# Block stack of sliding-window attention and a gated MLP: the opening loads, statistics and first tiles rearranged

## The chip, the cores and the metric

The kernel runs on one core of a Trainium2 chip. The metric is the device time of one execution in microseconds; lower is better. A core has five engines that are used here: TensorE (PE in the profile; its weight loads are the row PEld), VectorE (DVE), ScalarE (ACT), GpSimd (POOL) and SyncE (SP), which issues most of the transfers. Each engine works through its own list of instructions in order and waits on semaphores for the others.

## The reference

One layer norm feeds two branches, and their results meet at the end. S is 2048, D is 576, F is 4608, there are 32 heads of 18, and a query sees the last 256 keys.

```python
xn = _layernorm(x, axis=-1)            # eps = 1e-5, no scale or offset
s = _A_ref(xn, A_wqkv, A_wo)           # causal attention in a window of 256, 32 heads
g = _silu(_B_ref(xn, B_w_gate, B_w_up, B_w_down))
return x + s * g
...
# in _B_ref
g = jnp.einsum("bsd,df->bsf", x, w_gate)
u = jnp.einsum("bsd,df->bsf", x, w_up)
h = _sigmoid(g) * u
return jnp.einsum("bsf,fd->bsd", h, w_down)
```

## The kernel before

*Tiling.* The 2048 rows are four chunks of 512, each four blocks of 128 rows. D is split into a remainder of 64 and four pieces of 128. Every product runs as a pair of matmuls, one on rows 0 to 63 and one on rows 64 to 127 of the array (`pair`, line 123; `turn`, line 131). The gate and up projections of an F tile (128 columns of 4608, 36 tiles) are two operations: `f10` with the four large pieces and half the rows, `f11` with the other half and the remainder, which completes both sums.

*A planner sets the order.* The program first builds a graph of operations (`build_graph`, line 365). `schedule` (line 1125) then walks through time with an estimate for each operation, for the landing of each transfer and for the hand-over between engines, and picks for each engine the operation that can start soonest, a priority counting 10 ns a step (`PRIO_NS`). The list that results is what each engine runs; semaphores alone decide when. So a changed estimate changes the order of instructions, also far from the place where it is used. Attention (scores, exp, the product with V), the projections and the gate/up and down matmuls of several chunks are interleaved on TensorE in this way.

*The opening of chunk 0.* SP issues the four x blocks (`load_x`, line 418), then the gate and up weights of the first two F tiles (`wgs`, 256 columns each) and their remainders of 64 rows (`wgr`, 512 columns, for four tiles), then further weights. For each block the layer norm (`build_ln`, line 525) takes two half-row statistics on DVE (lines 541 and 543), aggregates them (545), adds eps (547), takes the power -0.5 on POOL (549), normalises on DVE (557), and copies 64 columns a second time (561), since the remainder is held twice. Ten small transposes on TensorE (`tr`, line 613) bring the block into PSUM, and one copy (590) into `xnT`. Block 2 has its statistics on ACT and POOL instead (`act_stats`, lines 600 to 604): a sum, a mean on POOL, a Square with that mean as bias, and again POOL. The PSUM copies of blocks 0, 1 and 2 are on ACT, that of block 3 on DVE (`XE_ENG`).

*Warm-up and early tiles.* TensorE runs 43 pairs of matmuls on zeros before the first transposes and ten more behind them (`warm`, line 490). The first two F tiles are early ones (`NEARLY`): each is computed in four slices of 128 columns of xnT, as the blocks come in; the first half of a third tile is held ready in a further PSUM unit (`ahead`, line 995).

*Runs.* The product with V (`f_pv`, line 804) runs for four groups of heads at a time as one unbroken run of 128 (chunk 0) or 192 small matmuls (the other chunks, line 817), eight runs in all. `fits` (line 1113) tells the planner where such a run may stand: it counts TensorE's instructions in blocks of 256 (`FETCH`), and asks that the time since the edge of the block before is at least `FETCH_NS`.

*Names.* `dma:x{i}` is the load of x block i, `dma:w:{c}:{wg}` that of a gate or up weight pair in chunk c, `dma:wgr` that of a remainder, `ln:*` the layer norm, `xe:{i}` the copy of block i from PSUM to `xnT`, `th` and `hm` the tanh and the product behind gate and up.

## Time and profile before

| what | value |
|---|---|
| median of the runs | 557.37 us (three: 557.37, 556.61, 557.46) |
| the profiled execution | 556.48 us; span from its first to its last instruction 555.2 us |
| granted TensorE clock in that execution | 1.00 |
| DMA | 75.87 MB, of which the queue of SP 68.71 MB |
| instructions fetched by the queue named instruction | 66 packets of 1.08 MB together (q8) |

The span is cut by the profile into forty slices for its busy digits. TensorE's are 8 in the first and the last slice and 9 in all others. In the first four slices the transfers run at 230 to 263 GB/s. Matmul rows overlap one another, because a matmul starts before the one ahead of it has left the array, so the distance from start to start tells more than the duration of a row. In a row of the timeline the first number is the start in us from the span's start, the second the duration, and what stands in brackets is the idle time of the engine before it and what ended that.

### The profile page before, as it was taken

How to read it: one execution, taken by the hardware profiler on the slowest of the kernel's cores; microseconds unless marked ns; L12 is line 12 of the kernel's file. 1: busy time of each engine (PE TensorE's matmuls, PEld its weight loads, DVE VectorE, ACT ScalarE, POOL GpSimd, SP SyncE). 2: the span in 40 equal slices, each digit the busy share in tenths (PEclk: the TensorE clock that was granted, in tenths of full speed). 3: DMA queues.
4: the chain of work that ended last, by engine and by line, in shares of the span. 5: the costliest groups of instructions: out<-in, count | busy, mean ns of one | idle time of the engine just before them, and what ended most of it. 6: DMA issues, size and time to landing. Idle time of an engine off the chain costs nothing.

```text
span 555.2 us, 19412 instructions
## 1 busy us (share of the span) xinstructions
PE 549.9 (99%) x8342; PEld 341.2 (61%) x8342; DVE 325.1 (59%) x782; ACT 271.7 (49%) x379; POOL 208.8 (38%) x360
## 2 busy tenths in 40 slices
PE   8999999999999999999999999999999999999998
PEld 7454455777555655577855565447877655445887
DVE  5467677745966545746565557664455657653511
ACT  4246554432566543645265563764165555765021
POOL 5634353826271230554452322745063332700300
DMA  8899999542256664462126653663013464540001
GB/s 230 234 263 239 248 241 257 150 91 59 72 164 182 198 167 132 129 161 53 32 65 193 201 162 101 185 179 87 9 34 103 119 204 138 153 134 2 20 28 46
DMA packets 141213, 75.87 MB, mean 137 GB/s; under 512 B 43676, under 2 KB 139260, under 8 KB 141128
## 3 DMA queue, kind: packets, MB, share of 16 engines
q1 hardware_dynamic: 133704, 68.71, 47.3%
q0 software_dynamic: 7424, 5.92, 4.0%
q8 instruction: 66, 1.08, 0.8%
q14 instruction: 19, 0.16, 0.1%
HBM read 63.18 MB, written 2.36 MB: 118 GB/s over the span
## 4 chain that ended last, share of the span: by engine, by line
PE 98%; DMA 1%; SPq 0%; issue 0%; DVE 0%; ACT 0%
PE ps L127 95%; PE ps L817 3%; DMA wgs<-in_B_w_up_dram 1%; SPq L290 0%; ACT thf L1087 0%; PE ps L613 0%; DVE thf L1089 0%; DVE xf L1092 0%
## 5 line engine op out<-in xcount | busy, mean ns | idle before, releaser
L127 PE MATMUL ps<-xnT,wgs 64*128 64x512 bf16 (+1 forms) x2400 | 284.0, 368 | 0.6 <-DMA wgs<-in_B_w_up_dram 0.5
L767 ACT ACTIVATE expr<-ps 128x1024 bf16<-128x1024 f32 (+4 forms) x160 | 155.0, 968 | 81.0 <-PE ps L127 80.5
L127 PEld LDWEIGHTS ps<-xnT,wgs 64*128 64x128 bf16 x2400 | 114.7, 94 | 108.6 <-issue 1.1
L127 PE MATMUL ps<-wd_sb,hT 64*128 64x288 bf16 (+2 forms) x2448 | 152.7, 276 | 0.0
L290 POOL DMA_DIRECT2D qk<-qd x160 | 82.9, 524 | 161.7 <-PE ps L127 152.9
L977 DVE SCALAR_TENSOR_TENSOR hT<-tring,ps 128x512 bf16<-128x512 bf16 x144 | 98.6, 685 | 74.2 <-ACT tring L974 72.6
L974 ACT ACTIVATE tring<-ps 128x512 bf16<-128x512 f32 x144 | 86.2, 598 | 113.9 <-PE ps L127 112.3
L127 PEld LDWEIGHTS ps<-wd_sb,hT 64*128 64x128 bf16 x2448 | 113.0, 94 | 29.4
L780 DVE TENSOR_TENSOR expr<-expr,mask 128x128 bf16<-128x128 bf16 (+2 forms) x240 | 65.2, 299 | 62.0 <-ACT expr L767 59.4
L290 POOL DMA_DIRECT2D oT<-o2T x72 | 36.8, 520 | 115.3 <-DVE ot L848 52.4
L731 POOL TENSOR_SCALAR kx<-kprev,small 128x256 bf16<-128x256 bf16 x64 | 60.1, 949 | 6.0 <-PE ps L127 5.1
L127 PE MATMUL ps<-qk,kx 64*128 64x320 bf16 (+1 forms) x704 | 59.2, 254 | 0.0
L127 PE MATMUL ps<-xnT,wgr 64*128 64x512 bf16 (+1 forms) x300 | 56.0, 367 | 0.0
L127 PEld LDWEIGHTS ps<-qk,kx 64*128 64x128 bf16 x704 | 31.9, 94 | 26.6
L127 PE MATMUL ps<-xnT,wqg 64*128 64x512 bf16 (+1 forms) x320 | 37.7, 355 | 0.0
L652 DVE CAST qd<-ps 128x1024 bf16<-128x1024 f32 (+1 forms) x20 | 22.3, 1115 | 11.1 <-PE ps L127 11.1
L845 DVE STREAM_TRANSPOSE ot<-ps 128x512 f32<-128x512 f32 x32 | 20.3, 687 | 13.9 <-PE ps L817 13.8
L127 PEld LDWEIGHTS ps<-xnT,wgr 64*128 64x128 bf16 x300 | 15.0, 94 | 16.4
L731 DVE TENSOR_SCALAR kx<-qk,small 128x512 bf16<-128x512 bf16 x64 | 21.9, 370 | 5.4 <-PE ps L127 4.9
L853 DVE STREAM_TRANSPOSE o2T<-o 128x512 bf16<-128x512 bf16 x32 | 22.6, 706 | 3.0 <-DMA oT<-o2T 2.5
L127 PEld LDWEIGHTS ps<-xnT,wqg 64*128 64x128 bf16 x320 | 15.0, 94 | 11.5 <-issue 0.4
L1080 ACT ACTIVATE thf<-ps 128x576 bf16<-128x576 f32 x12 | 7.8, 650 | 27.4 <-PE ps L127 27.4
(68 smaller groups left out, 289.3 us busy)
## 6 DMA issues: line engine op xcount, KB each, us to landing
wgs<-in_B_w_gate_dram SPq DMA_DIRECT2D x72, 256.0 KB, 3.5
wgs<-in_B_w_up_dram SPq DMA_DIRECT2D x72, 256.0 KB, 4.0
wd_sb<-in_B_w_down_dram SPq DMA_DIRECT2D x9, 576.0 KB, 6.7
wqg<-in_A_wqkv_dram SPq DMA_DIRECT2D x32, 128.0 KB, 3.8
qk<-qd POOLq DMA_DIRECT2D x100, 36.0 KB, 2.7
wgr<-in_B_w_gate_dram SPq DMA_DIRECT2D x36, 64.0 KB, 3.1
wgr<-in_B_w_up_dram SPq DMA_DIRECT2D x36, 64.0 KB, 2.9
wvo<-in_A_wqkv_dram SPq DMA_DIRECT2D x4, 576.0 KB, 4.2
```

The lines of the kernel that those rows point to most:

```text
L127: res = eng.matmul(outs[i], lhs(ROWS[t], i), rhs(ROWS[t], i), start=start, stop=stop, tile_position=(64 * t, 0))
L290: o = self.op(eng, DMA_ISSUE_NS[eng], lambda e: e.dma_start(dst, src), name, deps, prio, nbytes=nbytes)
L652: return eng.tensor_copy(dst, self.both(h, n))
L731: return e.tensor_scalar(self.kx[:, sx, pos:pos + n_ // SW, t, :], src.rearrange("p (s k) -> p s k", k=SW), self.half[:, t:t + 1], None, A ...
L767: return eng.activation(self.expr[:, se, :, lo * SW:NT], self.both(h, NT)[:, :, lo * SW:NT], ACTF.Exp, scale=SM_SCALE)
L780: return eng.tensor_tensor(e_, e_, m_, ALU.mult)
L817: res = eng.matmul(outs[i][p0:p0 + VH, cols], self.v_aug[ROWS[i], o:o + VH], self.expr[ROWS[i], se, t, cols], start=m == 0, stop=m == len( ...
L845: return e.transpose(self.ot1[:, p1, :], self.halves(hp, NT, un)[i])
L853: t2 = op("DVE", dve_ns(NT), lambda e, p2=p2, p3=p3: e.transpose(self.o2T[:, p3, :], self.o2[:, p2, :]), f"ot2:{c}:{pr}:{i}", deps=[on, d3 ...
L974: th = op("ACT", act_ns(NT), lambda e: e.activation(self.tring[:, st, :], bank(h, 0), ACTF.Tanh, scale=0.5), f"th:{c}:{ft}", deps=[pg, dt_ ...
L977: mu = op("DVE", dve_ns(NT), lambda e: e.scalar_tensor_tensor(self.hT[:, ft, :], self.tring[:, st, :], 1.0, bank(h, 1), ALU.add, ALU.mult) ...
L1080: th = op("ACT", act_ns(w), lambda e: e.activation(v2(t), y2(), ACTF.Tanh, scale=0.25), f"fth:{nm}", deps=[f2, dt_], prio=0)
```

## The change

- x block 0 is loaded in two transfers of 288 columns; blocks 1 and 2 follow; block 3 is issued behind the first gate and up weights and the first half of their remainder. That remainder is loaded in two halves of 256 columns.
- In chunk 0 (blocks 0, 1 and 3) eps is no longer added on DVE to the variance. GpSimd adds 576 eps to an entry of the first half's statistics before the aggregation, while DVE takes the second half.
- Block 2's statistics on ACT: the sum is taken with sign -1, and the Square uses it as its bias with scale 576, so that it needs nothing from POOL.
- The PSUM copy of block 0 moves from ACT to DVE.
- 41 warm-up pairs in place of 43, and none behind the first transposes.
- Three early F tiles in place of two; the third in slices of 384 and 128 columns. The held first half is that of the fourth tile, in a PSUM unit of its own (`pool_a`, unit 0).
- The planner: landing times of the opening's transfers come from a running count of bytes; some hand-over times, gaps between scores (`SPACE_NS`) and fill times differ; `fits` counts the time of a run from when the instructions before it could be taken up, with other bounds for three phases (`FETCH_NS`, `RUN_NEED`). So instructions change places in the whole program; TensorE has 24 warm-up matmuls fewer and 18 more for the slices of the third tile.

The core of the diff:

```diff
@@ -43,8 +43,12 @@
 FETCH = 256
 FETCH_AT = 193
 FETCH_AHEAD = 64
-FETCH_NS = (6200.0, 4350.0)
+FETCH_LEAD = 16
+QUEUED = 48
+FETCH_NS = (7800.0, 5700.0, 4250.0)
+RUN_NEED = (1.0, 1.0, 1.15, 1.0, 1.15, 1.0, 1.15, 1.0)
 RUN_NS = 6.3
+RELAX_NS = 100e3
 STEP_NS = (54.0, 30.6)
...
@@ -66,18 +70,24 @@
 NTH = 4
 NTAIL = 80
 LAST_STORES = 3
-LN_PRIO = (0, 0, 0, 16)
-X_PRIO = (0, 0, 0, 0)
-REM_PRIO = 0.6
+LN_PRIO = (10,0,10,60)
+X_PRIO = (0,.1,.2,.3,1.5)
+REM_PRIO = 0.3
+REM1_PRIO = 1.5
+LATE_PRIO = 1.9
+SPLIT = False
 STATS_ACT = (2,)
-APPLY_ACT = ()
 DUP_ACT = ()
-XE_ENG = ("ACT", "ACT", "ACT", "DVE")
-NWARM = (43, 10)
-NEARLY = 2
-FIRST_SLACK_NS = (-800.0, -1500.0)
+XE_ENG = ('DVE','ACT','ACT','DVE')
+NWARM = ((41,1),)
+HOLD = False
+NEARLY = 3
+OPEN_NS = 2000.0
+OPEN_BYTES_PER_NS = 270.0
+X_LAT_NS = (400.0, 400.0, 600.0, 700.0, 800.0)
+W_LAT_NS = (700.0, 800.0)
 BUSY_SLACK_NS = 1500.0
-PARTS = (((0, 1), (1, 2), (2, 3), (3, 4)),) * NEARLY
+PARTS = (((0, 1), (1, 2), (2, 3), (3, 4)),) * 2 + (((0, 3), (3, 4)),)
 NQK = 5
 
 DMA_ISSUE_NS = {"SP": 640.0, "POOL": 520.0, "ACT": 650.0}
...
@@ -88,10 +98,11 @@
 TURN_WAIT_NS = 235.0
 PE_OUT_NS = 210.0
 PE_IN_NS = 60.0
-POOL_IN_NS = 140.0
+POOL_IN_NS = 100.0
 DMA_PE_NS = 690.0
-FILL_NS = 100.0
-SPACE_NS = (1700, 1800, 1700, 1700)
+OPEN_PE_NS = 150.0
+FILL_NS = 80.0
+SPACE_NS = (1700, 2100, 1700, 2000)
 DMA_BYTES_PER_NS = 280.0
...
@@ -417,10 +430,13 @@
 
     def load_x(self, c, i=0):
         if c == 0:
-            for i in range(BPC):
-                self.x_dma[i] = (self.dma(self.x0[:, i, :], self.x[i * P:(i + 1) * P, :], P * D * 2, f"dma:x{i}", ("x0", i), prio=X_PRIO[i]),
-                                 self.x0[:, i, :])
-                self.x_dma[i][0].slack = -220.0
+            for n in range(BPC + 1):
+                i = max(n - 1, 0)
+                cs = slice(0, D) if n > 1 else slice(n * D // 2, (n + 1) * D // 2)
+                o = self.dma(self.x0[:, i, cs], self.x[i * P:(i + 1) * P, cs], P * (cs.stop - cs.start) * 2, f"dma:x{i}:{n}",
+                             ("x0", n), prio=X_PRIO[n])
+                o.lat = X_LAT_NS[n]
+                self.x_dma.setdefault(i, ([], self.x0[:, i, :]))[0].append(o)
             return
...
@@ -461,7 +477,9 @@
                          deps=[z], prio=0)
         self.warm_h = self.pool_f.hold()
         self.warm_src = zero
-        self.warm(NWARM[0], z, None, 107)
+        self.warm_last = None
+        for n, wide in NWARM:
+            self.warm(n, wide, z, self.warm_last, 100)
 
...
@@ -538,16 +556,17 @@
                 mean, rs = self.act_stats(x_in, o_x, pr)
                 ag = None
             else:
-                b1 = op("DVE", 390, lambda e, ss=ss, x_in=x_in: e.bn_stats(self.bnst[:, ss, 0, :], x_in[:, 0:288]),
-                        f"ln:bn1:{st}", deps=[o_x, ds], prio=pr)
-                b2 = op("DVE", 390, lambda e, ss=ss, x_in=x_in: e.bn_stats(self.bnst[:, ss, 1, :], x_in[:, 288:576]),
-                        f"ln:bn2:{st}", deps=[o_x, ds], prio=pr)
-                ag = op("DVE", 200, lambda e, ss=ss: e.bn_aggr(self.mv[:, ss, :], self.bnst[:, ss, :, :]),
-                        f"ln:ag:{st}", deps=[b1, b2], prio=pr)
-                ve = op("DVE", 140, lambda e, ss=ss: e.tensor_scalar(self.veps[:, ss, :], self.mv[:, ss, 1:2], EPS, None,
-                                                                    ALU.add), f"ln:ve:{st}", deps=[ag], prio=pr)
-                rs = op("POOL", 560, lambda e, ss=ss: e.tensor_tensor(self.rstd[:, ss, :], self.veps[:, ss, :],
-                                                                      self.neghalf[:, :], ALU.pow),
+                bs = self.bnst[:, ss, :, :]
+                b1, b2 = (op("DVE", 440, lambda e, bs=bs, x_in=x_in, n=n: e.bn_stats(bs[:, n, :], x_in[:, n * D // 2:(n + 1) * D // 2]),
+                             f"ln:bn{n}:{st}", deps=[o_x[min(n, len(o_x) - 1)], ds], prio=pr) for n in range(2))
+                var = self.mv[:, ss, 1:2]
+                if c == 0:
+                    b1 = op("POOL", 230, lambda e, bs=bs: e.tensor_scalar(bs[:, 0, 2:3], bs[:, 0, 2:3], EPS * D, None, ALU.add), f"ln:ep:{st}",
+                            deps=[b1], prio=pr)
+                ag = ve = op("DVE", 210, lambda e, ss=ss, bs=bs: e.bn_aggr(self.mv[:, ss, :], bs), f"ln:ag:{st}", deps=[b1, b2], prio=pr)
+                if c:
+                    ve = op("DVE", 140, lambda e, var=var: e.tensor_scalar(var, var, EPS, None, ALU.add), f"ln:ve:{st}", deps=[ag], prio=pr)
...
@@ -582,8 +595,6 @@
                 return self.transposes(eng, h, lambda r, o: self.xnr[r, sn, o:o + P])
             tr = op("PE", KB * 29.5, f_tr, f"tr:{st}", deps=[ap, dup, self.op_ident, war], prio=0, acq=h, ni=20)
             self.r_xn.release(sn, tr)
-            if i == 0:
-                self.warm(NWARM[1], None, tr, 80)
 
...
@@ -597,11 +608,11 @@
         op = self.op
         junk = self.tring[:, :, :].rearrange("p t n -> p (t n)")[:, 0:D]
         sx, nm, sq, ve = (self.act_st[:, k:k + 1] for k in range(4))
-        a1 = op("ACT", act_ns(D) + 150, lambda e: e.activation(junk, x_in, ACTF.Identity, accum_out=sx), "ln:as", deps=[o_x, self.op_tab], prio=pr)
-        m = op("POOL", 150, lambda e: e.tensor_scalar(nm, sx, -1.0 / D, None, ALU.mult), "ln:am", deps=[a1], prio=pr)
-        a2 = op("ACT", act_ns(D) + 150, lambda e: e.activation(junk, x_in, ACTF.Square, bias=nm, accum_out=sq), "ln:aq", deps=[m], prio=pr)
-        v = op("POOL", 150, lambda e: e.tensor_scalar(ve, sq, 1.0 / D, EPS, ALU.mult, ALU.add), "ln:av", deps=[a2], prio=pr)
-        rs = op("POOL", 560, lambda e: e.tensor_tensor(self.arstd[:, :], ve, self.neghalf[:, :], ALU.pow), "ln:ar", deps=[v, self.op_negh], prio=pr)
+        a1 = op("ACT", act_ns(D) + 190, lambda e: e.activation(junk, x_in, ACTF.Identity, scale=-1.0, accum_out=sx), "ln:as", deps=[o_x, self.op_tab], prio=pr)
+        a2 = op("ACT", act_ns(D) + 290, lambda e: e.activation(junk, x_in, ACTF.Square, bias=sx, scale=float(D), accum_out=sq), "ln:aq", deps=[a1], prio=pr)
+        m = op("POOL", 230, lambda e: e.tensor_scalar(nm, sx, 1.0 / D, None, ALU.mult), "ln:am", deps=[a1], prio=pr)
+        v = op("POOL", 290, lambda e: e.tensor_scalar(ve, sq, 1.0 / D ** 3, EPS, ALU.mult, ALU.add), "ln:av", deps=[a2], prio=pr)
+        rs = op("POOL", 560, lambda e: e.tensor_tensor(self.arstd[:, :], ve, self.neghalf[:, :], ALU.pow), "ln:ar", deps=[v, m, self.op_negh], prio=pr)
         return nm, rs
...
+            by = [[self.load_nat(self.wgs[:, sw, :, i, a:b], w[:, fc][:, a:b], f"dma:w:{c}:{wg}:{a}", ("w", sw, i, a), pr + later, [dw, self.op_xnT[0][0] if HOLD and c == 0 and wg == 1 else None])
+                   for i, w in enumerate((self.wg, self.wu))] for a, b, later in cuts]
+            ds = [d for g in by for d in g]
             if wg % 2 == 0:
                 f8 = slice(wg * WG * P, (wg + 2) * WG * P)
                 sr, dr = self.r_wr.produce()
                 rslots[wg // 2] = sr
-                self.op_wgr[wg] = self.load_rem(self.wgr[:, sr, :], (self.wg[:, f8], self.wu[:, f8]), f"dma:wgr:{c}:{wg}",
-                                                ("wgr", sr), pr + (REM_PRIO if c == 0 and wg == 0 else -0.5), [dr])
-            rem = self.op_wgr[wg - wg % 2]
+                first = c == 0 and wg == 0
+                self.op_wgr[wg], self.op_wgr[wg + 1] = [
+                    self.load_rem(self.wgr[:, sr, a * P:b * P], [w[:, f8][:, a * P:b * P] for w in (self.wg, self.wu)], f"dma:wgr:{c}:{wg}:{a}",
+                                  ("wgr", sr, a), pr + late, [dr])
+                    for a, b, late in (((0, WG, REM_PRIO), (WG, 2 * WG, REM1_PRIO)) if first else ((0, 2 * WG, -0.5),))] * (1 if first else 2)
+            rem = self.op_wgr[wg]
...
@@ -992,7 +1009,7 @@
                 for part in range(len(PARTS[ft])):
                     lo = gate_up(ft, h, 0, None if part else h, part, [u])
                     if ft == early - 1 and part == len(PARTS[ft]) - 1:
-                        ahead = self.pool_f.hold()
+                        ahead = (self.pool_a if NEARLY > 2 else self.pool_f).hold()
...
@@ -1110,14 +1127,25 @@
             waits[key] = max(waits.get(key, -1), d.idx)
         return {key: v for key, v in waits.items() if known.get(key, -1) < v}
 
-    def fits(self, at, n, st, places, ffn):
+    def fits(self, at, o, st, places, now, rate, waited):
+        n = o.run
+        need = RUN_NEED[sum(int(v) << 1 - j for j, v in enumerate(o.name.split(":")[1:3]))]
         def when(p):
             if p < at:
-                return next(t0 + (p - a0) * w for a0, t0, w in reversed(places) if a0 <= p)
-            return st + TURN_NS + min(p - at, n) * RUN_NS + max(p - at - n, 0) * STEP_NS[ffn]
+                return next((t0 + (p - a0) * w, kind) for a0, t0, w, kind, held in reversed(places) if a0 <= p)
+            return st + TURN_NS + min(p - at, n) * RUN_NS + max(p - at - n, 0) * rate, now
         edge = at + (FETCH_AT - at) % FETCH
         while edge - FETCH - FETCH_AHEAD < at + n:
-            if edge > at and when(edge) - when(edge - FETCH - FETCH_AHEAD) < FETCH_NS[ffn]:
+            p = edge - FETCH - FETCH_LEAD
+            t0, kind = when(p - QUEUED)
+            for a0, _, _, _, held in reversed(places):
+                if a0 < p - FETCH:
+                    break
+                if a0 <= p:
+                    t0 = max(t0, held)
+            if p >= at:
+                t0 = max(t0, st)
+            if edge > at and when(edge)[0] - t0 < FETCH_NS[kind] * (need - waited / RELAX_NS):
                 return False
```

`FETCH_NS` has bounds for chunk 0, for later chunks, and for stretches with little gate and up work left. `SPLIT` and `HOLD` are False and have no effect.

## The prediction

> **What bounds the kernel now.** I read the page first: its span, its busy times, and the chain that ended last.
>
> ```profile
> span 555.2 us, 19412 instructions
> PE 549.9 (99%) x8342; PEld 341.2 (61%) x8342; DVE 325.1 (59%) x782; ACT 271.7 (49%) x379; POOL 208.8 (38%) x360
> ...
> PE 98%; DMA 1%; SPq 0%; issue 0%; DVE 0%; ACT 0%
> ```
>
> TensorE is the chain. Then the list of who waited for whom, for TensorE alone, and the chain in order of time:
>
> ```profile
> PE ps L613 <- DVE xnr L561: 1.1, 2, 0.8
> PE ps L127 <- DVE small L459: 1.1, 1, 1.1
> PE ps L127 <- DMA wgs<-in_B_w_up_dram: 0.5, 1, 0.5
> ```
>
> ```profile
> 3.14 4.71 DMA wgs<-in_B_w_up_dram
> 7.84 0.14 issue
> 7.98 1.00 PE ps L127 x26
> ```
>
> All waits of the whole execution, 2.7 us, lie before 8 us: nothing later makes TensorE wait for another engine or a transfer. From 7.98 us on it does needed work without a break, so the time is the start of that work plus its length. What fixes the start stands in the timeline:
>
> ```profile
> 2.88 0.46 DVE L541 BATCH_NORM_STATS2 small<-x 128x6 f32<-128x288 bf16 x1 [1.88 <-DMA x<-in_A_x_dram]
> 3.98 0.15 DVE L547 TENSOR_SCALAR small<-small 128x1 f32<-128x1 f32 x1
> 4.58 0.68 ACT L600 ACTIVATE tring<-x 128x576 bf16<-128x576 bf16 x1 [2.29 <-DMA x<-in_A_x_dram]
> 4.83 0.43 DVE L557 TENSOR_SCALAR xnr<-x,small 128x576 bf16<-128x576 bf16 x1
> 5.54 0.32 PE L613 MATMUL ps<-ident,xnr 64*128 64x64 bf16 x10 [0.33 <-DVE xnr L561]
> 5.72 0.78 ACT L602 ACTIVATE tring<-x,small 128x576 bf16<-128x576 bf16 x1 [0.36 <-POOL small L601]
> 6.49 0.68 ACT L590 ACTIVATE xnT<-ps 128x640 bf16<-128x640 bf16 x1
> 7.18 0.32 PE L613 MATMUL ps<-ident,xnr 64*128 64x64 bf16 x10 [0.76 <-DVE xnr L561]
> 7.98 0.95 PE L127 MATMUL ps<-xnT,wgs 64*128 64x128 bf16 x24 [0.48 <-DMA wgs<-in_B_w_up_dram]
> 10.62 0.49 DVE L590 COPY xnT<-ps 128x640 bf16<-128x640 bf16 x1 [0.22 <-PE ps L613]
> ```
>
> The reader should see three gates close behind one another: block 0's copy to xnT on ScalarE ends at 7.17 (it waited for ScalarE, busy with block 2's statistics), block 1's transposes end at 7.50, and the up weights land at 7.84.
>
> **The opening after the change, by these rows.**
> *x in halves.* The stretch from 4.40 to 5.50 us moves 274 GB/s, so half of x0 (73.7 KB) is 0.27 us: its statistics can start at 2.61 instead of 2.88. The other half is issued where x1 was; its end lies between 2.86 (same bytes) and 1.25 + 2.08 = 3.33 (x0's own issue to use, from 0.80 to 2.88). The two statistics follow at 0.38 us (2.88 to 3.26), so I take 3.0 to 3.44; the late end, 3.3 to 3.75, is swallowed below, since DVE then waits for x1 (about 4.0) anyway.
> *eps on GpSimd.* L547 goes from DVE (0.15 us, three times, and the hand-over after it); the new operation is nearest to GpSimd's 0.23 us of L601. For x0 it lies beside the second statistics: free. If that cover were gone it would cost 0.23 + 0.09 (DVE's 4.13 to GpSimd's 4.22). Aggregate 3.48 to 3.69, pow 0.57 from 3.78 to 4.35.
> *DVE's new order* puts both statistics of x1 and its aggregate ahead of block 0's normalisation: 4.0 to 4.82, x1's eps waits on GpSimd for the pow (4.55 to 4.78), aggregate to 5.08. So normalisation 5.12 to 5.55, copy of 64 columns to 5.77, transposes 5.83 to 6.15: 0.29 later than now. Next on DVE is block 1's normalisation (its pow ends 5.74) to 6.24, then the moved copy to xnT.
> *First PSUM copy on DVE.* ScalarE would be busy till 6.25 (below) and takes 0.68; DVE's row for the same copy is 0.49: 6.28 to 6.77. With 0.08 to TensorE the first useful matmul can start at 6.85. Behind the copy waits block 1's 64-column copy (6.99) and so transposes tr:1 at 7.05, which now stand behind the first matmuls.
> *Weights.* With x3 behind them 147 KB less lie ahead: 0.54 us. The last of the transfer's 16 completions at 7.84 goes to 7.30, use at 7.44; the other fifteen had come by 6.97, so 6.43 and 6.57. The late one held a 512-byte packet of 1.00 us, against a median of 0.03, the only such packet before 24 us. I take it as chance: the copy decides, 6.85; 7.44 is kept for the range.
> *Bytes and issues behind.* SP issues x3 ninth, about 5 us; it lands by some 7.8 and is wanted at 7.95, after block 2. The first remainder goes as two 256-column halves, two more issues of 0.55 us ahead of the third weight pair, which landed at 11.6 and 12.4 and is not used before 15. The second pair's last completion (10.47) meets the third early tile at 10.2: 0 to 0.3 us, I take 0.1.
> *ScalarE statistics.* The Square no longer waits for L601: 0.37 us earlier (5.35 against 5.72); block 2's transposes at 8.0 follow the tile-0 and tile-1 work of block 0 without a gap.
> *Third early tile.* Four slices become 384 + 128 columns instead of one 512: nine more small pairs of 2.7 ns, 0.02 us. It fills the time in which x3 is normalised.
>
> From 7.98 to the end of the fourth and fifth tiles' work at 17.26 TensorE now needs 9.28 us, 0.21 of it small waits. After: the same work, plus tr:1 (0.15) and 0.02, with 0.1 + 0.2 of waits, so 9.54: 6.85 + 9.54 = 16.39. Gain in the opening: **0.87 us** (0.28 with the late weights).
>
> **The rest of the kernel.** Runs of attention matmuls are re-placed; the count of matmuls stays. What can be won there is what is lost now: of the eight runs one is longer than its sisters,
>
> ```profile
> 336.21 2.69 PE L817 MATMUL ps<-expr,v_aug 64*19 64x320 bf16 x192
> ```
>
> against 2.47 for the same 192: 0.22 us. In the trace an instruction block of 16 KB arrives 1 us before that stop ends. The Trainium skill (Runtime: NRT & Kernel Launch, Instruction fetch mechanics) says that instructions are streamed in such blocks and that the crossing is mostly hidden; by it this part would be worth nothing, by the row 0.22.
> A loss: where the second half of a tile's gate/up work directly follows its own first half, it stands still a moment:
>
> ```profile
> 87.20 2.13 PE L127 MATMUL ps<-xnT,wgs 64*128 64x512 bf16 x16
> 89.17 0.38 PE L127 MATMUL ps<-xnT,wgr 64*128 64x512 bf16 x2
> ```
>
> 1.97 us from row to row, against 1.73 (18.33 to 20.06) elsewhere: 0.24. The old order has one such place, the new order two (tile 35 of chunk 0, tile 0 of chunk 1): +0.24. The planner also counts on PSUM 40 ns sooner after its release; TensorE's list has no wait for ScalarE at all, so between 0 and 65 groups x 0.04 = 2.6 us (95 of the 160 exp waited for TensorE, the other 65 could be waited for); nearest is nothing, I take 0.2.
>
> **Sum.** -0.87 - 0.22 + 0.24 + 0.20 = -0.65 us. The profiled execution took 556.48 (span 555.2), so it would be 555.8; the median of the runs is 0.89 above that execution. I apply the difference to the median: **556.7 us**, -0.12%. A measurement of this kernel tells about 0.2%, 1.1 us, from no change (three runs spread over 0.85).
>
> **Rivals.**
> *The late weights come again* (chance 0.15): a gain of 0.28 - 0.22 = 0.06: 557.3. For it: several packets of 0.4 to 0.7 us between 2.8 and 6.7 us. Against: only one of 1 us.
> *The spread goes too* (0.27): if the 0.89 us between profiled run and median is a wait that these steps remove, 557.37 - 0.65 - 0.89 = 555.8. For: the first packets of x and w vary by about that. Against: the profiled execution, too, paid for late weights.
> *Instruction fetch becomes the wait* (0.13; the slower side): each run of attention takes in 384 TensorE instructions in 2.47 us. If the new places leave the fetch too little time, each of eight loses 0.22 or more, as one does now; eight lose 1.76, with the sum without its -0.22 this is 557.37 - 0.43 + 1.76 = 558.7. It turns the sign from two on. Against: seven of eight are clean now, and the two runs of chunk 0 move to where few loads run.
> *TensorE starts cold* (0.10). The first 64 warm-up matmuls take 3.4 us, the next 28 take 0.81 (busy time from 4.40 to 5.50): the clock doubles near 4.4. After, 82 of them end near 4.9 and no more follow tr:0. If the doubling comes after they end, or is lost in the two pauses of 0.7 to 0.9 us before 6.85, 3.35 us of work run at half: +1.6, 558.3. Against: pauses of 0.33, 0.76 and 0.48 us are survived now. The Trainium skill (TensorE: Matmul & The Clock Gate, The HAM clock gate) says the window of about 3.4 us runs freely, so the moment varies from run to run; the 3.35 us here agrees in size, and one trace cannot show the variation.
>
> **How the numbers follow.** Forecast 0.35, rivals as given. Faster by over 0.2% (below 556.26): the second rival and a little of the forecast's own spread, 0.31. Slower by over 0.2% (above 558.48): most of the fetch rival and a third of the cold start, 0.16. Within: 0.53. The forecast's own range is 556.3 to 557.2; with the other cases 555.7 to 558.4.
>
> **What would show it.** First matmul on xnT and wgs at 6.8 to 6.9 us, released by DVE's copy; a release by the up weights near 7.4 shows the first rival. x0's first statistics at 2.6; tr:0 about 5.8, later than now. No idle of TensorE after 8.2. All eight runs of 192 (128 in chunk 0) at 2.47 (1.86). Two stops of 0.24 in gate/up work. It is wrong if the first small pairs follow at 0.107 instead of 0.056 us, or if waits appear after 20 us.

## The result, and the profile after

The changed kernel took 559.68 us in the median of 10 runs (558.12 to 563.64), the kernel before beside it 556.87 (556.48 to 557.68, 10 runs). The ratio is 1.0059, 95% interval 1.0042 to 1.0076: slower by about 0.6%, where 556.7 us was predicted and 558.4 was the upper end of the range. The profiled execution took 562.57.

The page of the changed kernel first: its span, TensorE's busy time, the clock granted to TensorE in 40 slices, and the shares of the chain that ended last.

```profile
span 561.2 us, 19413 instructions
PE 552.3 (98%) x8336; PEld 347.8 (62%) x8336; DVE 325.3 (58%) x780; ACT 270.9 (48%) x378; POOL 210.0 (37%) x363
...
PEclk8999999899999999999999999999999999999999
...
PE 97%; DMA 2%; DVE 0%; SPq 0%; POOL 0%; issue 0%; ACT 0%; DVEq 0%
```

The span is 6.0 us longer, TensorE is busy 2.4 us longer although it issues six matmuls fewer, and two slices of the clock row, the first and the eighth, are below 9. The waits in TensorE's list add up to 6.4 us, against 2.7 before; the 2.4 us of busy time are matmuls that ran more slowly, net of the 24 warm-up matmuls that are gone. Who waited for whom, for TensorE alone (total, times, longest):

```profile
PE ps L138 <- DMA wd_sb<-in_B_w_down_dram: 2.8, 1, 2.8
PE ps L624 <- DVE xnr L580: 1.4, 1, 1.4
PE ps L138 <- DVE small L475: 1.0, 1, 1.0
PE ps L138 <- DVE xnr L580: 1.0, 1, 1.0
PE ps L138 <- PE ps L138: 0.2, 1, 0.2
```

The first line is new: before, nothing made TensorE wait after 8 us; now a down-projection weight tile does, once, for 2.8 us. The next three lie in the opening, and the last is the stop in the second chunk's first gate/up tile, one of the two turns that the prediction priced. The opening's timeline (start, duration, then engine, line and operation; in brackets the idle time ahead of it and what ended that):

```profile
2.89 0.46 DVE L560 BATCH_NORM_STATS2 small<-x 128x6 f32<-128x288 bf16 x1 [1.89 <-DMA x<-in_A_x_dram]
3.45 0.24 POOL L564 TENSOR_SCALAR small<-small 128x1 f32<-128x1 f32 x1 [1.65 <-DVE small L560]
3.79 0.46 DVE L560 BATCH_NORM_STATS2 small<-x 128x6 f32<-128x288 bf16 x1 [0.44 <-DMA x<-in_A_x_dram]
4.36 0.21 DVE L566 BATCH_NORM_AGGREGATE small<-small 128x2 f32<-128x12 f32 x1
5.59 0.38 DVE L576 TENSOR_SCALAR xnr<-x,small 128x576 bf16<-128x576 bf16 x1
6.24 0.32 PE L624 MATMUL ps<-ident,xnr 64*128 64x64 bf16 x10 [1.35 <-DVE xnr L580]
6.78 0.48 DVE L601 COPY xnT<-ps 128x640 bf16<-128x640 bf16 x1
7.58 0.61 PE L138 MATMUL ps<-xnT,wgs 64*128 64x128 bf16 x8 [1.02 <-DVE xnr L580]
```

The steps stand in the predicted order, and the addition of eps on GpSimd (0.24 us) is hidden for block 0, as predicted. But the second half of x's first block landed at 3.77 us, so the aggregate starts 0.9 us later than forecast (4.36 against 3.48), and the first gate/up matmul starts at 7.58, not 6.85. The windows view shows what that did (stretch, its length, then busy time and count for PE, PEld, DVE, ACT, POOL; granted clock; DMA share; GB/s):

```profile
4.40:7.80 3.40, 1.03 (x34) 0.76 (x30) 2.45 (x9) 1.65 (x4) 2.57 (x6) 0.94 0.90 243
7.80:11.20 3.40, 3.40 (x86) 3.40 (x83) 2.31 (x9) 1.41 (x2) 0.87 (x4) 0.56 0.78 219
11.20:14.60 3.40, 3.39 (x91) 2.75 (x87) 0.70 (x9) 0.00 (x0) 3.29 (x3) 1.00 0.86 231
...
102.90:105.70 2.80, 0.04 (x2) 0.00 (x0) 1.72 (x6) 0.62 (x1) 0.81 (x2) 1.00 1.03 283
105.70:109.20 3.50, 3.46 (x36) 2.37 (x38) 0.56 (x3) 0.92 (x1) 1.79 (x4) 0.60 0.23 58
```

Twice the same pair of lines: a stretch in which TensorE has little to do (1.03 of 3.40 us, 0.04 of 2.80), and behind it one of the same length at about half clock (0.56, 0.60). The trace's clock records put the half clock from 7.39 to 10.81 and from 106.38 to 109.79, 3.41 us each. In the first of them the gate/up pairs follow one another at 0.107 us instead of 0.056. Set matmul by matmul against the trace of e7_x0 (below), whose list of matmuls is the same, needed work takes 1.4 us more in the first window and 1.7 us more in the second.

For the second place, TensorE's list and the list of SP's queue around it:

```profile
102.29 0.65 PE L138 MATMUL ps<-wd_sb,hT 64*128 64x288 bf16 x8
105.74 1.53 PE L138 MATMUL ps<-wd_sb,hT 64*128 64x288 bf16 x16 [2.80 <-DMA wd_sb<-in_B_w_down_dram]
```

```profile
85.97 4.52 SPq L307 DMA_TRANSPOSE xnT<-xnr  x2
...
92.99 1.05 SPq L302 DMA_DIRECT2D wqg<-in_A_wqkv_dram  x2
94.09 2.58 SPq L302 DMA_DIRECT2D wqgr<-in_A_wqkv_dram  x2
...
98.45 0.48 SPq L302 DMA_DIRECT2D wd_sb<-in_B_w_down_dram  x1
```

The ninth and last piece of the down weights is issued at 98.45 and lands at 105.70. Before, it was issued here, landed at 96.90 and was first used at 102.31:

```profile
89.88 0.48 SPq L290 DMA_DIRECT2D wd_sb<-in_B_w_down_dram  x1
```

So the load is issued 8.6 us later than before: it now stands on SP's queue behind the two transposes, the next chunk's gate/up weights and its query/key weights. Its first use hardly moved; without the wait it would have come near 102.8. The attention run of chunk 0 has moved behind the gate/up work, so the first down products begin earlier (96.7 against 97.9, for all the time lost before).

### The profile page after: what moved, and what is told of

The parts are those of the page before. It is cut to its first block, busy times and chain, and to the rows that moved or that the text cites. A ratio compares the mean times of both kernels' runs of the same rounds, so it can differ in the third digit from the quotient of the medians.

```text
span 561.2 us, 19413 instructions
## 1 busy us (share of the span) xinstructions
PE 552.3 (98%) x8336; PEld 347.8 (62%) x8336; DVE 325.3 (58%) x780; ACT 270.9 (48%) x378; POOL 210.0 (37%) x363
## 4 chain that ended last, share of the span: by engine, by line
PE 97%; DMA 2%; DVE 0%; SPq 0%; POOL 0%; issue 0%; ACT 0%; DVEq 0%
PE ps L138 94%; PE ps L828 3%; DMA wd_sb<-in_B_w_down_dram 1%; DMA x<-in_A_x_dram 0%; SPq L302 0%; POOL small L569 0%; PE ps L624 0%; DVE small L560 0%; DVE small L566 0%; DVE xnr L576 0%; DVE xnT L601 0%; ACT thf L1104 0%; DVE thf L1106 0%; DVE xf L1109 0%; POOL small L564 0%
## 5 line engine op out<-in xcount | busy, mean ns | idle before, releaser
L138 PEld LDWEIGHTS ps<-xnT,wgs 64*128 64x128 bf16 x2416 | 119.4, 95 | 106.5 <-DVE xnr L580 1.1
L138 PE MATMUL ps<-wd_sb,hT 64*128 64x288 bf16 (+2 forms) x2448 | 155.2, 277 | 2.8 <-DMA wd_sb<-in_B_w_down_dram 2.8
L910 ACT ACTIVATE s_attn<-ps 128x576 bf16<-128x576 f32 x16 | 10.3, 650 | 20.5 <-PE ps L138 20.4
```

The costliest lines, as they stand in the source:

```text
L138: res = eng.matmul(outs[i], lhs(ROWS[t], i), rhs(ROWS[t], i), start=start, stop=stop, tile_position=(64 * t, 0))
L910: return eng.activation(dst, self.both(h2, 288), ACTF.Copy, scale=1.0 if c == NC - 1 else 0.25)
```

## The experiments

All are edits of one of the two kernels. Most change the finished lists of operations just before the program is written out, so that nothing else is planned anew; `place(b, engine, name, ahead_of)` takes one operation of an engine's list out and puts it ahead of another. Measured, each against runs of the kernel before on the same chip (medians 556.72 to 556.93). The ratio goes by the means of the runs, so it can lie apart from that of the medians:

| Label | Built on | Edit | Median us (runs) | Ratio to before, 95% |
|---|---|---|---|---|
| e1_wd8 | changed | ninth down load early | 557.71 (11) | 1.0012 (1.0004 to 1.0021) |
| e2_warm | changed | longer warm-up | 558.90 (10) | 1.0064 (1.0036 to 1.0091) |
| e3_both | changed | e1 and e2 | 557.07 (11) | 1.0003 (0.9994 to 1.0012) |
| b1_small | before | shorter warm-up | 558.28 (10) | 1.0024 (1.0015 to 1.0033) |
| e4_w44 | e1 | 44 warm-up pairs | 558.31 (6) | 1.0029 (1.0018 to 1.0040) |
| e5_w53 | e1 | 53 warm-up pairs | 558.59 (8) | 1.0030 (1.0020 to 1.0040) |
| e6_whole | e5 | x's first block whole | 557.52 (11) | 1.0014 (1.0006 to 1.0023) |
| b2_late | before | ninth down load late | 557.59 (12) | 1.0024 (1.0010 to 1.0039) |
| e7_x0 | e1 | x's first block whole | 556.29 (11) | 0.9995 (0.9986 to 1.0003) |
| e8_w55 | e6 | 55 warm-up pairs | 559.22 (9) | 1.0048 (1.0029 to 1.0066) |
| e9_turns | e7 | two matmul groups exchanged | 556.33 (11) | 0.9992 (0.9984 to 1.0001) |
| b3_halves | before | x's first block in halves | 558.03 (12) | 1.0023 (1.0012 to 1.0034) |
| e10_turn | e7 | one matmul group exchanged | 556.54 (11) | 0.9993 (0.9984 to 1.0002) |
| e11_x0only | changed | x's first block whole | 559.89 (12) | 1.0058 (1.0029 to 1.0086) |
| a2_after | changed | none | 561.84 (6) | 1.0087 (1.0059 to 1.0116) |

### The late load and the clock

The theory: the time went into a wait for the ninth down-weight load and into two windows of half clock. The rival: into the new order of the opening, or into the re-placed runs.

e1_wd8 moves the load forward, ahead of the next chunk's first remainder:

```
+    place(b, "SP", "dma:wd8", "dma:wgr:1:0:0")
```

> The changed kernel with one transfer moved: SP issues the last down weights (wd8) ten places earlier, right behind the block transposes of chunk 1; every other order is as in the changed kernel. Theory A (two causes: the last down weights are issued too late behind SP's queue, and the thin warm-up lets the TensorE clock fall for one window of 3.41 us): the 2.8 us wait of TensorE for wd_sb goes, and with it the second slow window (1.7 us); the opening's slow window stays where it was. Median 557.8 to 558.6, granted clock never below 0.997. Rival B (the loss is in the re-placed attention runs and their instruction fetch): no change, about 559.7.

e2_warm makes the last ten of the 41 warm-up pairs 384 columns wide, with as many instructions as before:

```
+    warms = [o for o in b.prog["PE"] if o.name.startswith("warm:")]
+    for o in warms[-10:]:
+        o.fn = b.f_wide
```

> The changed kernel with the last ten of its 41 warm-up pairs on 384 columns in place of 128, the count of instructions unchanged. Theory A: TensorE works to about 6.0 us, the window behind the warm-up is over half busy and the clock stays full: the first gate/up pairs follow at 0.056 us, not 0.107. The wait for wd_sb near 103 us stays. Median 558.0 to 559.0, granted clock 1.000 or 0.997, never 0.994. Rival C (the clock has no part; the opening is late because of its loads alone): no change, about 559.7.

e3_both has both edits.

> Both edits at once: the last down weights ten places earlier on SP, and the last ten warm-up pairs on 384 columns. Theory A: granted clock 1.000 in all runs, no TensorE wait after the opening, median 556.0 to 556.8, that is level with the kernel before or up to 0.9 us faster. If a third cause is at work (instruction fetch, or PSUM released later than planned) it stays above 557.5.

b1_small carries the clock half to the kernel before: the last 22 of its 53 warm-up pairs get 16 columns.

```
+    for o in warms[31:]:
+        o.fn = b.f_small
```

> The kernel before with the last 22 of its 53 warm-up pairs cut to 16 columns, the count and order of instructions unchanged, so that TensorE is about as little busy between 4.4 and 7.8 us as in the changed kernel. Theory A: in some or all runs the clock falls for one window, granted clock 0.997, and these runs take about 1.7 us more: median 557.0 to 558.6. Rival C (no part of the clock): within 0.3 us of the kernel before, clock 1.000.

The early load takes the wait away and 1.97 us off the median. Both edits together come to the kernel before (557.07), not below it, as 556.0 to 556.8 would have been. In b1_small TensorE was busy for 1.57 us of the stretch from 4.0 to 7.4 (2.31 in the kernel before), and the same groups that take 0.95 us there take half as much again; its timeline:

```profile
7.63 1.47 PE L127 MATMUL ps<-xnT,wgs 64*128 64x128 bf16 x24
...
9.80 1.49 PE L127 MATMUL ps<-xnT,wgs 64*128 64x128 bf16 x24
...
12.01 1.38 PE L127 MATMUL ps<-xnT,wgs 64*128 64x128 bf16 x24
```

The slow pairs go on to 13 us and cost 1.5 us in the median: the emptier opening alone does it, without the change. The way there is another one, though. The transposes at 5.74 and 7.37 already run at half pace (0.047 us from pair to pair, 0.029 in the kernel before), so nothing in this trace shows the full clock before its first clock record, which begins at 13.17 us: the clock did not fall after the warm-up, as in the changed kernel, but had not risen. (The windows view gives the stretch before that record a clock of 1.00; the distance between matmuls is the surer reading.)

e2_warm shows a price of the cure: the wide pairs ran into the time of the transposes and put the first gate/up matmul at 7.94. The wait for the ninth load stays, 1.8 us in its trace. Four of its ten runs had a granted clock of 0.994 to 0.997 and took 562.1 to 565.0; I had expected none at 0.994, and no trace shows where their half clock lies.

b2_late carries the other half over: the ninth down load goes ten transfers later in the kernel before.

```
+    place(b, "SP", "dma:wd8", "dma:wgr:1:2")
```

> The kernel before with one load moved: the ninth down-weight load goes ten transfers later on SP's queue (issue about 98 instead of 89.9 us). Theory 'the late down weights cost twice': they land near 105 us, TensorE waits 2 to 3 us for them at about 102.3, and the half-empty clock window is followed by one of 3.4 us at half clock: +3.5 to +4.7, 560.3 to 561.5. Rival 'the wait alone': +2 to +3 with the pairs behind it at full clock, 558.8 to 559.8. Rival 'the wait fills a pause that is there anyway': within 0.3 of the kernel before.

```profile
104.53 2.14 PE L127 MATMUL ps<-wd_sb,hT 64*128 64x288 bf16 x32 [1.86 <-DVE small L541]
```

The load landed at 104.39, the matmul started at 104.53: the wait is for the load, and the engine named in the bracket had long been done. The pairs behind it kept the full clock in this trace. The median rose by 0.7 us only, but two of the twelve runs, with a granted clock of 0.997, took 560.7 and 561.2: the wait without half clock is the usual case here. The transplant shows the wait, in a smaller size than I expected; that half clock can follow it is only to be inferred from the granted clock of those two runs.

### A stop that no engine explains

e1_wd8 and e3_both left something in the opening. Before the third early tile TensorE stands still, and the trace names no one (e1_wd8):

```profile
13.00 0.82 PE L138 MATMUL ps<-xnT,wgs 64*128 64x384 bf16 x8 [2.15 <-issue]
```

The tile's weights had landed at 10.90, and TensorE's semaphore instruction that waits for them was over at 10.98, two microseconds ahead of the restart: it was not a wait for data. What came later was a packet of the instruction queue (page of the changed kernel):

```profile
q8 instruction: 66, 1.08, 0.8%
```

66 packets of 16 KB, each the next 256 of TensorE's instructions. Counting instructions, a block begins exactly at the third early tile; its packet ran from 10.39 to 11.55 in e1_wd8, 1.45 us ahead of the restart. The next three kernels change how early that block is asked for, by more warm-up pairs.

```
-NWARM = ((41,1),)
+NWARM = ((44,1),)        # e4_w44; 53 in e5_w53, 55 in e8_w55
```

> The changed kernel with the ninth down-weight load early and 44 instead of 41 warm-up pairs of 128 columns, planned anew (the list of matmuls stays as it was up to the third chunk). The twelve added instructions let TensorE pass its 193rd instruction in the first transposes (about 6.1 us) instead of at the first gate/up matmul (7.25). Theory 'instruction fetch in the opening': the block that begins at the third early tile then arrives by about 9.3 us instead of 11.5, the stop of 2.15 us before that tile (profile of the early load alone) goes or stays under 0.5, and the time falls from 557.7 to 555.9 to 556.7, unless the clock falls in the opening (the warm-ups keep TensorE busy for only about 40% of the window from 3.98 to 7.39): then small gate/up pairs follow at 0.107 us up to 10.8 and the time is 557 to 558. Rival 'the stop is a wait for data': it stays at 0.8 to 2.2 us and the time at 557.1 to 557.7.

> The same with 53 warm-up pairs, all ahead of the first transposes (about 5.6 us instead of 4.9), planned anew. Now the window from 3.98 to 7.39 is some 57% busy, as in the kernel before, and instruction 193 is passed among the warm-ups, at about 5.2 us. Theory 'clock and fetch in the opening': no pair at 0.107 us after 7.4, no stop before the third early tile, no wait for the last down weights: 555.6 to 556.3, below both kernels. Rival 'what is left over after the early load lies in the rest of the kernel (the new places of the attention runs, the order of the gate/up work)': 556.9 to 557.7 with a clean opening.

The stop before the third early tile went in both, as its theory said, and both became slower than e1_wd8. In e4_w44:

```profile
9.27 0.40 PE L138 MATMUL ps<-xnT,wgs 64*128 64x128 bf16 x8 [1.48 <-issue]
```

The instruction packet now ran from 6.52 to 8.13, among the first weights, and one of the 16 parts of the remainder load came at 9.18 where the other 15 had come by 7.26; the matmul waited for that one (here the semaphore instruction itself took 1.75 us). In e5_w53 the same: packet 6.46 to 8.02, last part at 9.06, a stop of 0.69. The stop had only changed its cause. In the plans made anew one attention run grew as well, by 0.14 us in e4_w44 and 0.49 in e5_w53. So the clean opening that e5_w53 was to test did not come about, and neither of its two theories is settled by it.

### x's first block whole

e6_whole and e7_x0 load x's first block in one transfer again; everything behind it is issued 0.47 us earlier.

```
+    a.fn = lambda e: e.dma_start(b.x0[:, 0, :], b.x[0:P, :])
+    sp.remove(c)                      # c: the second half
+    for o in b.ops:
+        o.deps = [a if d is c else d for d in o.deps]
```

> The same as with 53 warm-up pairs, but x's first block again in one load. Theory 'the two halves cost more than they give': the whole block landed at 2.86 us in the kernel before, its second half at 3.77 in the changed one; so the aggregate of block 0 ends about 3.8 instead of 4.4, the first transposes start at 5.6 to 5.8 instead of 6.2, the first gate/up matmul up to 0.6 us earlier (7.0 instead of 7.5), and the time is 0.3 to 0.6 us lower than with halves. Rival 'another gate takes over' (the up weights landed at 7.34, block 1's statistics stand ahead of block 0's normalisation on VectorE): the first gate/up matmul moves by 0.2 us or less and the time stays within 0.2.

> The changed kernel with the ninth down-weight load early and x's first block in one load; warm-ups (41 pairs) and all other lists as they are. Against the early load alone (557.71). Theory 'the halves cost the opening': block 0's first transposes at 5.3 to 5.5 us instead of 5.97, first gate/up matmul at 6.6 to 6.8 instead of 7.25. TensorE passes its 193rd instruction there, so its instruction block can be there some 2 to 3 us + 1.0 + 1.4 later, 11.0 to 12.2, where the third early tile would start at 10.1: a stop of 0.9 to 2.1 us at that tile stays (the gain is eaten there), and the time is 557.0 to 557.7. Rival 'the fetch is not tied to instruction 193 but to the clock time of the opening's transfers': the packet comes at the same 10.4 to 11.5 and the stop grows to 2.5 or more: no gain at all, 557.7. Rival 'no stop': 555.9 to 556.4.

e6_whole took 1.07 us less than e5_w53 (0.3 to 0.6 expected), e7_x0 1.42 less than e1_wd8. For e7_x0 I had expected no gain, since the instruction block would still be late. Its timeline:

```profile
6.96 0.40 PE L138 MATMUL ps<-xnT,wgs 64*128 64x128 bf16 x8 [0.63 <-DVE xnT L601]
...
10.66 0.82 PE L138 MATMUL ps<-xnT,wgs 64*128 64x384 bf16 x8
```

The up weights landed at 6.38 instead of 7.00 in e1_wd8, the first matmul starts 0.29 us earlier, and the stop before the third early tile is 0.2 us instead of 2.15, because the packet ran from 8.31 to 9.35. In the four traces with 41 warm-up pairs and x whole it starts at 8.31 to 8.80, in the five with halves at 8.99 to 10.39: it comes sooner where the loads do. Why it does was not tested. The gain does not come from earlier statistics: the aggregate of block 0 starts at 4.00 us here, at 3.85 in e1_wd8.

b3_halves does this part of the change alone, in the kernel before:

```
+    a.fn = lambda e: e.dma_start(b.x0[:, 0, 0:288], b.x[0:P, 0:288])
+    c = b.dma(b.x0[:, 0, 288:576], b.x[0:P, 288:576], P * 288 * 2, "dma:x0b", ("x0", 9))
+    sp.insert(sp.index(a) + 1, c)
```

> The kernel before with one part of the change alone: x's first block in two loads of 288 columns, one issue more at the head of SP's queue; each statistic waits for its half. Theory 'the additional issue puts the whole opening back': every later load is issued 0.45 us later, the second half lands at 3.2 to 3.8 us, the up weights at 7.3 to 8.3, the first gate/up matmul starts at 7.9 to 8.4 instead of 7.5 to 8.0, and the time is 0.3 to 1.5 us above the kernel before. Rival 'the halves are free, or help': within 0.2 us of it or below.

It cost 1.2 us in the median, inside what the theory of the additional issue gave. The one trace, of a run at 556.98, shows only 0.11 us of it, the first gate/up matmul at 8.09 instead of 7.98. Four of the twelve runs had a granted clock of 0.997 and took 558.4 to 560.1; the other eight have a median of 557.5, 0.7 above the kernel before. So a half-clock window is part of the price, but no trace caught one, and the rest stays open.

e8_w55 was to remove the last stop by instructions, in an attention run:

> As the kernel with 53 warm-up pairs and x's first block in one load (557.52), with 55 pairs, planned anew; this plan's shortest way between two instruction blocks around the last attention run is 2.3 us instead of 1.7. Theory 'what is left over is instruction fetch': the stop of 0.5 us in the last attention run goes, the opening stays as it was (first gate/up matmul 6.9 to 7.0, 0.4 at the third early tile), and the time is 556.3 to 557.0, at or just below the kernel before (556.9). Rival 'the plan's other parts make the difference': 557.3 to 557.8 with every run of 192 at 2.47.

It did the opposite. The planner put the runs elsewhere, and another one met a late block:

```profile
PE ps L828 <- issue: 1.8, 1, 1.8
```

### Matmul groups exchanged

e9_turns puts other work between the two halves of a tile at the two places where the change has them back to back; e10_turn does only the first.

```
+    place(b, "PE", "f2:0:0:0", "f11:0:35")
+    place(b, "PE", "f2:3:1:8", "f11:1:0")     # e9_turns only
```

> The kernel with the early down-weight load and x's first block in one load (556.29), with two matmul groups of TensorE's list exchanged: the first down product goes between the two halves of the last tile of the first chunk, and the last down product of that chunk between the two halves of the second chunk's first tile. Theory 'a half that directly follows its own other half stops TensorE': the stops of 0.24 and 0.33 us go, and the time is 555.6 to 555.9, below the kernel before. Rival 'the stop follows the last tile wherever it stands' (a PSUM bank that comes free late): the excess of 0.24 and 0.33 stays in the same groups, or shows in the groups put between, and the time is 556.2 to 556.4.

> The early down-weight load, x's first block in one load, and only the first of the two exchanges (the first down product between the two halves of tile 35). The other exchange had put 0.41 us in front of the second chunk's next tile. Theory 'the stop goes and nothing comes back': -0.24 against the version without the exchange (556.29): 555.9 to 556.2, below the kernel before. Rival 'it is below what the runs tell apart': 556.2 to 556.5.

Around the first place, in e9_turns:

```profile
93.14 1.03 PE L138 MATMUL ps<-xnT,wgs 64*128 64x512 bf16 x8
94.01 0.65 PE L138 MATMUL ps<-wd_sb,hT 64*128 64x288 bf16 x8
94.50 1.03 PE L138 MATMUL ps<-xnT,wgs 64*128 64x512 bf16 x8
```

At this place the stop of 0.24 us is gone and nothing comes back: against e7_x0, TensorE gains 0.24 us here in both traces. So it belongs to a half that directly follows its own other half. At the second place the stop of 0.33 goes too, but 0.41 us come back at the next tile, 0.23 of it a wait for VectorE (L1098); there the stop only moved, much as the rival had it. The medians did not move (556.33 and 556.54 against 556.29): in these two traces the stop before the third early tile was 0.5 and 0.9 us, 0.22 in e7_x0, and such scatter is larger than what the exchange gives.

### Do the two causes add?

e11_x0only loads x whole and leaves the ninth down load where the change has it; a2_after is the changed kernel once more.

> The changed kernel with x's first block in one load and nothing else; the ninth down-weight load stays where the change has it. Theory 'two causes that add': the opening is that of the version with both repairs (first gate/up matmul near 6.9, pairs at 0.056), the wait for the last down weights stays at 1.8 to 3.5 us and can halve the clock behind it: 556.3 + 2 = 557.8 to 559.0. Rival 'the late down weights only hurt after a late opening': with the earlier opening the wait grows, as SP's queue does not move, or the wait vanishes, time outside this.

> The changed kernel itself once more, for a second trace. If the low clock in the opening is a matter of chance (where the windows fall), this one can show pairs at 0.056 us behind 7.6, and then a stop of 0.8 to 2.1 us at the third early tile as in the kernels with the early load; the wait for the last down weights is there in either case, at 1.8 to 3.5 us. Median again 558.5 to 560.5.

No gain of x whole alone is to be seen: its median is 559.89, and with the early load as well it is 3.6 us lower. But the changed kernel's own two medians, 559.68 and 561.84 (558.5 to 560.5 expected), lie 2.2 us apart, so these medians cannot show whether the two repairs add. The trace shows how what it wins can be lost. The wait and the windows of e11_x0only:

```profile
PE ps L138 <- DMA wd_sb<-in_B_w_down_dram: 4.0, 1, 4.0
```

```profile
101.00:105.60 4.60, 0.67 (x12) 0.31 (x8) 2.39 (x7) 1.02 (x1) 1.98 (x4) 0.84 1.01 290
105.60:109.00 3.40, 3.36 (x30) 2.22 (x32) 0.00 (x0) 0.84 (x1) 0.61 (x2) 0.50 0.55 132
```

The load lands at 105.59 us here, at 105.70 in the first trace of the changed kernel and at 104.60 in the second. It does not follow TensorE; what an earlier opening wins is waited away at this load, and half clock lasts for two windows (104.16 to 110.99 in the clock records).

The changed kernel, e1_wd8, e2_warm, e3_both, e7_x0 and e11_x0only run the same list of 8336 matmuls, so their traces can be set against each other matmul by matmul. In us later than e7_x0, from start to start (so a wait counts a little more than the idle time in brackets):

| Trace | behind the opening | added by the wait for the ninth load | added by the half clock behind it | at the last matmul |
|---|---|---|---|---|
| changed, first | 1.80 | 2.97 | 1.68 | 6.46 |
| changed, second | 1.10 | 2.57 | 1.69 | 5.37 |
| e11_x0only | 0.53 | 4.14 | 2.60 | 7.28 |
| e2_warm | 0.88 | 1.94 | 0.01 | 2.83 |
| e1_wd8 | 2.34 | 0.00 | 0.00 | 2.34 |
| e3_both | 1.27 | 0.00 | 0.00 | 1.28 |

Everywhere else the distances stay the same to 0.05 us or better, and e7_x0 itself ends 0.45 us before the kernel before. So the re-placed runs, the first rival, hold no loss of this size: the opening and this one load hold all of it, and the load's place decides more.

The second trace of the changed kernel had no half-clock window in the opening, but the stop at the third early tile, and the half-clock window at 105 again:

```profile
11.76 0.82 PE L138 MATMUL ps<-xnT,wgs 64*128 64x384 bf16 x8 [1.16 <-issue]
```

So the slow opening of the first trace is not there in every execution, and where it is absent the instruction stop takes part of its place.

## Why the prediction was wrong, point by point

*"Nothing later makes TensorE wait."* This is the step that failed. It is true of the trace of before, and I carried it over to the changed kernel, of which I had said myself that instructions change places in the whole program. I asked for the new places of the attention runs, but not for those of the loads: SP's queue was costed in the opening only. The ninth down load had 5.4 us to spare before (landing at 96.90, use at 102.31). After, it is issued 8.6 us later for a use at nearly the same time, and TensorE waits 2.4 to 2.8 us for it. With the half clock behind it this place costs 4.3 to 4.7 us in the two traces of the changed kernel, and moving the load gave 1.97 us in the median.

*"TensorE starts cold"* (chance 0.10, +1.6). The mechanism and its size were right: pairs at 0.107, 1.4 to 1.7 us for a window; the changed kernel's first trace shows the clock lost in the pauses, b1_small a rise that came too late. It was missed that it needs no opening: waits of 2.4, 2.8 and 4.0 us brought it near 105 us. The chance was too low.

*First matmul at 6.85, a gain of 0.87.* The order of the steps was right, the sizes were not. The second half was to land between 2.86 and 3.33, with a late end that would be swallowed; it landed at 3.16 to 3.77 in the traces of this change, and in the first trace it was not swallowed: block 0's normalisation starts at 5.59, not at 5.12. The start was 7.58 in the first trace and 7.00 in the second. The weights' gain was worked out from bytes (147 KB less ahead of them, 0.54 us), but the half block took the issue that the fourth block left: the up weights are issued at 3.14 us as before, and landed at 7.34 and 6.75. With x whole they are issued at 2.67 and landed at 6.25 to 6.51.

*Third early tile, 0 to 0.3 us from its weights.* With 41 warm-up pairs it did stop, for 0.2 to 2.15 us in the traces without half clock in the opening, but for its instructions. *"Instruction fetch becomes the wait"* was a rival for the eight attention runs; these stayed clean in both traces of the changed kernel, and the fetch showed where I had not looked for it.

*The turn: +0.24.* Right in kind: the sizes were 0.24 and 0.33, so +0.33 net instead of +0.24. e9_turns removes the first; the second only moves.

*The fetch stall of one attention run: -0.22.* The stall is gone in the changed kernel, as predicted (its block had come 1.35 us before the stop ended, not 1); the PSUM release (+0.20) left no wait that the traces name.

What the change could have been shows in e7_x0: in its profile TensorE's last matmul group starts 0.45 us before that of the kernel before, and its median is 0.4 us lower, close to the -0.65 of the sum. The interval of that ratio (0.9986 to 1.0003) still takes in 1, as do those of e9_turns and e10_turn; none of them is shown to beat the kernel before, and all three beat the changed kernel by over 3 us.

Open: how the 2.8 us of the median divide between the wait, the windows and the instruction stop in the runs that were not profiled; and why the packets of e1_wd8 took so long. The granted clocks give a hint at the first: of the changed kernel's sixteen runs the three at 1.000 took 558.3 to 559.7 us, the nine at 0.997 (the size of one window) 558.1 to 563.8, the four at 0.994 (two) 562.6 to 565.0.

## What to carry to other kernels

When a plan is made anew, list every load, where it now stands on its queue and when its first user starts: the slack of the old plan says nothing of the new one, and a gain ahead of a late load can be waited away there. Price a wait of TensorE of 2 us or more by what follows it, too. And in the opening every issue at the head of the queue moves the loads behind it; in these traces the instructions came later as well.

## What the runs showed of the hardware

- **The granted clock changes in steps of 3.413 us whose place varies from execution to execution.** In nine of the ten traces with clock records the full clock begins between 3.98 and 6.83 us, in b1_small at 13.17; inside the kernel a stretch of half clock lasts 3.413 or 6.827 us. Where the records give a window's place, TensorE's busy time in it goes with what followed: from full clock, 0.64, 0.92, 1.00 and 1.23 us of 3.41 were followed by half clock, 1.74 to 2.83 by full; from half clock, 1.8 to 2.5 were followed by half, 2.9 to 3.4 by full.
- **TensorE restarts 1.30 to 1.48 us after the end of its instruction packet.** Eight traces have the stop at the border of a block: packet ends at 9.22, 9.35, 9.66, 9.89, 9.95, 10.36, 10.61 and 11.55 us, restarts at 10.67, 10.66, 11.05, 11.19, 11.43, 11.76, 11.94 and 13.00.
- **One of the 16 parts of a load can be 1 to 2.5 us later than the other 15.** In several openings this begins with an instruction packet among the loads (e4_w44: 7.26 for 15 parts, 9.18 for the last). In e1_wd8 and in the kernel before it began earlier, and in four other openings with such a packet no part is over 0.7 us late, so the packet alone does not explain it.
